# Order of the upper FFN products, of their PSUM banks and of their weight transfers in a fused attention and SwiGLU kernel

## The chip, the cores and the metric

The kernel runs on one core of one Trainium2 chip. The time is the device time of one execution in microseconds (us). The core's engines work from queues of their own: TensorE (PE; its weight loads are listed as PEld), VectorE (DVE), ScalarE (ACT), GpSimd (POOL) and SyncE (SP). GpSimd computes almost nothing here; it issues most of the transfers between the chip's memory (DRAM) and the on-chip memory (SBUF). Results of TensorE go to PSUM, of which this kernel uses eight banks.

## The reference

```
q, k, v: (4, 8, 768, 64); proj: (64, 6); w_gate, w_val: (512, 1536); w_out: (1536, 512)
q_bucket, k_bucket = 6 sign bits of q @ proj, k @ proj
scores = q @ k.T / 8 where the buckets agree, else -1e9
attn = softmax(scores) @ v                        # (4, 8, 768, 64)
x = attn.transpose(0, 2, 1, 3).reshape(3072, 512)
g = x @ w_gate
out = (g * sigmoid(g) * (x @ w_val)) @ w_out      # (3072, 512), float32
```

The FFN weights come as float64 (seen by the kernel as pairs of 32-bit words) and are narrowed on the chip.

## The kernel before

**Attention.** The work is cut into 16 pairs of heads (4 batches of 4), and each pair into two halves of 384 query columns. A half is a unit: first a score section of 36 matmuls (`score`, L491: for each of six key chunks and each of two heads two passes of the float32 product and one product of hash signs that does the masking), with 12 exponentials on ScalarE (L494), then 24 matmuls with `v` (`attend`, L506). VectorE adds the exponentials for the denominators (L520, L524). `norm` (L557) scales the finished rows of x later.

**FFN, upper part.** While the attention of one batch runs, the FFN of the batch before is put between its units, some atoms after each. `up_strassen` multiplies x (512 by 768 tokens) with w_gate and w_val in blocks. One call of `both(i)` is a block of work here: it makes two of the twelve column tiles of the hidden layer, for gate (g = 0) and value (g = 1). It uses the Strassen-Winograd form: seven products n = 0 to 6 for each g, with weights A11, S1, S2, A12, S3, S4 and A22, that accumulate on PSUM banks: n = 0, 2, 4, 6 on bank a, n = 1, 5 on bank b, n = 3 on bank c. Gate and value have a bank each, so there are a0, a1, b0, b1 (0 for gate, 1 for value). A product is four matmul instructions of 384 columns. After n < 3 ScalarE copies the bank to SBUF (L660), after n = 3, 4, 5 VectorE adds the bank to that copy (`plus`, L585), and after n = 6 the bank itself is the result. What is complete goes through `finished`: for the gate a tanh on ScalarE (L567) and a combination on VectorE (L568), for the value the gating on VectorE (L572). These wait in the list `later` for one or two steps (`settle`). After n = 6 they read the PSUM bank directly, after n = 5 the copy in SBUF.

**Nested blocks.** In batches 1 to 3 (`nested`) the product n = 3 is itself done by seven inner products of 192 columns (`deeper`, in four calls go = 0 to 3, on banks c, d and e), with inner weights that `weigh` makes on VectorE from A12. The calls go = 2 and go = 3 accumulate on d and each is read by VectorE. A batch has six blocks; batch 0 (not nested) runs them in the first part of the span, batches 1 and 2 between units, batch 3 in one go at the end.

**Order of work.** The order is written out by hand: `todo` lists the products of each step, `step(at)` issues a step, and each engine runs its queue in that order. Banks come from a pool of seven (`bank`), shared by score sections, upper blocks and down products.

**Weights.** In batch 0 the weights are still being prepared. `load_words` (L278) has GpSimd fetch 512 KB pieces of w_gate, w_val and later w_out; `scale_to` (L293, L294) works on them on ScalarE, `narrow` (L307, L309, L312) on VectorE; `form` makes the sums S1 to S4 (L341) and stores the seven blocks of a tile in DRAM: A11 and A12 (L333), A22 (L335), and the sums in two stores per tile (L345). `bring` (L323) fetches the blocks of a tile for its use into `places[g]`: go = 0 fetches S2, S1, A11, go = 1 the other four. `free` calls it as soon as the products that read the old blocks are done, so each transfer waits in GpSimd's queue for TensorE. Steps of preparation are put between the steps of the blocks (`prepare_on`, `scale_ahead`).

**FFN, down part.** `down_strassen` multiplies the hidden layer with w_out, on banks named c, b, a; its sums of hidden tiles (L585) for a batch's first chunk are begun ahead of the last upper step (`early`).

Of the kernel before, what the change touches and what calls it, by code (L numbers as in the profile page):

```python
# [18 lines left out]
def kernel(  # L19
# [11 lines left out]
    nc = tc.nc  # L31
# [3 lines left out]
    P = 128  # L35
# [157 lines left out]
    NB4 = PIECE // P  # L193
    BL = 2 * P
    NB = 7
    PARTS = [slice(0, 3), slice(3, NB)]
    S2, S1, A11, A12, S3, S4, A22 = range(NB)
    ram = [dram.tile([P, NB, BL], FP32, tag=f"ram{i}", name="ram") for i in range(NG)]
    STAGE = NJ * PIECE
    PAD = 4 * AW - NFP * HD  # L200
# [26 lines left out]
    formed = part(8 * BL, at=down_at).rearrange("p (g x m) -> p g x m", g=2, m=BL)  # L227
# [90 lines left out]
    def bring(k, go):  # L318
        if k < B * NG:
            if k < NG:  # L320
                while k not in summed:
                    next(preparing)
            nc.gpsimd.dma_start(places[k % 2][:, PARTS[go], :], ram[k % NG][:, PARTS[go], :])  # L323

    def form(n):

        blocks = stages[n % 2].rearrange("p k (g r m) -> p g k r m", g=2, m=P)
        a11, a12, a21, a22 = (blocks[:, :, 2 * k : 2 * k + 2, r, :]
                              for r in range(2) for k in range(2))
        group = [n // 2 * NB4 + 2 * pair + n % 2 for pair in range(2)]  # L330
        for pair, i in enumerate(group):
            w = stages[n % 2][:, :, 2 * pair * P : 2 * (pair + 1) * P]
            nc.gpsimd.dma_start(  # L333
                ram[i][:, A11 : A12 + 1, :].rearrange("p n (j m) -> p (n j) m", m=P), w[:, :, 0:P])
            nc.gpsimd.dma_start(ram[i][:, A22, :].rearrange("p (j m) -> p j m", m=P),  # L335
                                w[:, 2:4, P : 2 * P])
        s2, s1, s3, s4 = (formed[:, :, x, :].rearrange("p g (j m) -> p g j m", m=P)
                          for x in range(4))
        for o, x, y, op in ((s3, a11, a21, ALU.subtract), (s2, a22, s3, ALU.subtract),
                            (s1, s2, a11, ALU.add), (s4, a12, s2, ALU.subtract)):  # L340
            nc.vector.tensor_tensor(o, x, y, op=op)  # L341
            yield True
        for pair, i in enumerate(group):
            for at, x in ((S2, 0), (S3, 2)):
                nc.gpsimd.dma_start(ram[i][:, at : at + 2, :], formed[:, pair, x : x + 2, :])  # L345
            summed.add(i)
            if i < 2:
                for go in range(2):
                    bring(i, go)

    def prepare():
# [235 lines left out]
    def up_strassen(x, b, first):  # L587
# [16 lines left out]
        nested = b > 0  # L604
# [5 lines left out]
        def both(i):  # L610


            f = 2 * i
            k0 = b * NG + 2 * i
            now = [{}, {}]
            later = []
            done = [set(), set()]
            inner = {}

            def tile_of(g, spot):  # L620
                m, half = spot
                t = gate_tile() if g == 0 else hidden(f + m, half)
                now[g][spot] = t
                return t

            def settle(at):
                while later and later[0][0] <= at:
                    later.pop(0)[1]()

            def finished(g, spot, c, at, wait):  # L630
                if g == 0:
                    then = gate(tile_of(0, spot) if spot not in now[0] else c, c)
                else:
                    then = lambda: gated(hidden(f + spot[0], spot[1]), now[0][spot], c)
                later.append((at + wait, then))

            def free(g, n):
                done[g].add(n)
                if done[g] >= {0, 1, 2} and n in (0, 1, 2):
                    bring(k0 + 2 + g, 0)  # L640
                if len(done[g]) == NB:
                    bring(k0 + 2 + g, 1)

            def outer(n, g, at):
                my = now[g]
                block, to, xs = (
                    (A11, "a", [x[j][:, lo] for j in range(2)]),
                    (S1, "b", [x[j][:, hi] for j in range(2)]),
                    (S2, "a", [t2[:, j] for j in range(2)]),
                    (A12, "c", [x[2 + j][:, lo] for j in range(2)]),  # L650
                    (S3, "a", [t3[:, j] for j in range(2)]),
                    (S4, "b", [x[2 + j][:, hi] for j in range(2)]),
                    (A22, "a", [t4[:, j] for j in range(2)]),
                )[n]
                w = places[g][:, block, :].rearrange("p (j m) -> p j m", m=P)
                c = my[to]
                product(c, [(w[:, j], xs[j]) for j in range(2)], n in (0, 1, 3))
                spot = ((0, 0), (1, 1), (0, 1), (0, 0), (1, 1), (0, 1), (1, 0))[n]
                if n < 3:
                    nc.scalar.copy(tile_of(g, spot), c)  # L660
                elif n < 6:
                    plus(my[spot], my[spot], c)
                    c = my[spot]
                settle(at)
                if n >= 3:
                    finished(g, spot, c, at, 1 if n == 6 else 2)
                free(g, n)

            v11, v12, v21, v22 = (places[g][:, A12, j * P : (j + 1) * P]
                                  for g in range(2) for j in range(2))
            r1, r2, r3 = (inner_w[:, k] for k in range(3))
            r4 = v21

            def weigh():
                for o, p, q, op in ((r3, v11, v21, ALU.subtract), (r2, v22, r3, ALU.subtract),
                                    (r1, r2, v11, ALU.add), (r4, v12, r2, ALU.subtract)):
                    plus(o, p, q, op)

            def deeper(go, at):
                tg, tv = now[0][0, 0], now[1][0, 0]
                for w, to, xs, start, t, part in (
                    ((v11, "d", xl[:, 0], True, tg, 0), (r1, "e", xl[:, 1], True, tv, 1),
                     (v12, "c", xr[:, 0], True, tg, 0)),
                    ((r2, "d", u2, False, tg, 1), (r4, "e", xr[:, 1], False, tg, 1)),
                    ((r3, "d", u3, False, tv, 1),),
                    ((v22, "d", u4, False, tv, 0),),
                )[go]:
                    c = inner[to]  # L690
                    product(c, [(w, xs)], start)
                    t = t[:, part * HH : (part + 1) * HH]
                    plus(t, t, c)
                if go == 1:
                    finished(0, (0, 0), tg, at, 2)
                if go == 3:
                    finished(1, (0, 0), tv, at, 2)
                    for g in range(2):
                        free(g, 3)


            order = (0, 3, 1, 2, 4, 5, 6) if b == 0 and i == 0 else range(NB)
            todo = [[(n, g)] for n in order if n != 3 or not nested for g in range(2)]
            if nested:
                for go in range(4):
                    todo[6 + go].append(go)

            def step(at):
                if at == 0:
                    if nested:  # L710


                        names = [(inner, "d"), (now[0], "b"), (now[1], "b"), (now[0], "a"),
                                 (now[1], "a"), (inner, "e"), (inner, "c")]
                        for where, name in names:
                            where[name] = bank("up")[:, 0 : HH if where is inner else HQ]
                    else:
                        for name in "cba":
                            for w in range(2):
                                now[w][name] = bank("up")[:, 0:HQ]  # L720
                    while first:
                        first.pop(0)()
                if nested and at == 4:
                    weigh()
                for what in todo[at]:
                    if isinstance(what, tuple):
                        outer(*what, at)
                    else:
                        deeper(what, at)
                if at == len(todo) - 1:  # L730
                    settle(at + NB)

            for at in range(len(todo)):
                size = 2 if nested and at in (6, 7) else 1
                atoms.append((size, lambda at=at: step(at), at == len(todo) - 1))
# [103 lines left out]
    for u in range(0, N, NCH):  # L839
        n, half, _ = units[u]  # L840
# [103 lines left out]
```

## Time and profile before

The median of three runs is 998.54 us (998.32 to 999.62); the profiled execution spans 998.8 us.

| stretch, us | what runs | PE busy | DVE busy | ACT busy | DMA share |
|---|---|---|---|---|---|
| 0 to 106.9 | attention of batch 0, weights | 104.36 | 87.17 | 91.36 | 0.78 |
| 106.9 to 287.7 | attention of batch 1, upper FFN of batch 0, weights | 176.90 | 150.92 | 91.70 | 0.60 |
| 358.3 to 526.5 | attention of batch 2, upper FFN of batch 1 | 168.20 | 100.69 | 68.06 | 0.36 |
| 601.0 to 769.2 | attention of batch 3, upper FFN of batch 2 | 168.20 | 100.72 | 68.07 | 0.32 |
| 833.7 to 940.9 | upper FFN of batch 3 alone | 107.20 | 52.57 | 29.30 | 0.28 |
| 940.9 to 998.8 | down FFN of batch 3 alone | 54.78 | 16.96 | 4.47 | 0.08 |

The stretches left out are down products, partly beside attention. Busy times are us within the stretch. A busy TensorE row says that matmuls were in flight, not that they followed each other at full pace, so the time of a section of equal work is the better measure. In the profile's lines, a tile is named by the program's names: `up` and `po` are banks of the upper and down products, `sc` of the scores, `room` is the large SBUF tile with the weights, `ram` the formed weights in DRAM, `c` and `hid` the gate and hidden tiles.

### The profile page before, as it was taken

How to read it: one execution, taken by the hardware profiler on the slowest of the kernel's cores; microseconds unless marked ns; L12 is line 12 of the kernel's file. 1: busy time of each engine (PE TensorE's matmuls, PEld its weight loads, DVE VectorE, ACT ScalarE, POOL GpSimd, SP SyncE). 2: the span in 40 equal slices, each digit the busy share in tenths (PEclk: the TensorE clock that was granted, in tenths of full speed). 3: DMA queues.
4: the chain of work that ended last, by engine and by line, in shares of the span. 5: the costliest groups of instructions: out<-in, count | busy, mean ns of one | idle time of the engine just before them, and what ended most of it. 6: DMA issues, size and time to landing. Idle time of an engine off the chain costs nothing.

```text
span 998.8 us, 12932 instructions
## 1 busy us (share of the span) xinstructions
PE 989.2 (99%) x4705; PEld 618.0 (62%) x4705; DVE 608.8 (61%) x1066; ACT 397.3 (40%) x885; POOL 107.6 (11%) x212
## 2 busy tenths in 40 slices
PE   9999999999999999999999999999999999999998
PEld 4444555455576775556557776565556787666687
DVE  5898888678973625666564554655667442545531
ACT  7999555366323214444342223334443211222200
POOL 3222233131000000000000000000000000111000
PEclk9999999999999999999999999999999999999999
DMA  8777585786213033423331304233212011332101
GB/s 234 225 250 222 156 262 173 202 271 162 77 50 76 22 85 108 93 82 99 99 96 33 70 17 117 80 91 108 74 59 77 22 37 53 115 107 77 39 28 37
DMA packets 120944, 106.98 MB, mean 107 GB/s; under 512 B 89456, under 2 KB 104272, under 8 KB 120880
## 3 DMA queue, kind: packets, MB, share of 16 engines
q0 software_dynamic: 19296, 73.28, 22.7%
q1 hardware_dynamic: 100784, 32.67, 14.1%
q8 instruction: 37, 0.61, 0.2%
q10 hardware_dynamic: 800, 0.20, 0.1%
q14 instruction: 27, 0.22, 0.1%
HBM read 81.79 MB, written 17.30 MB: 99 GB/s over the span
## 4 chain that ended last, share of the span: by engine, by line
PE 91%; DVE 2%; ACT 2%; DMA 2%; issue 1%; POOL 0%; DVEq 0%; ACTq 0%; POOLq 0%
PE up L581 41%; PE po L581 22%; PE sc L491 15%; PE av L506 11%; DMA room<-in_moe_w_out_dram 1%; PE sum L537 1%; PE hps L409 1%; DVE acc L524 1%; PE tps L393 1%; ACT A L494 1%; ACT room L494 0%; DMA proj<-in_proj_dram 0%; DVE room L365 0%; ACT kb L414 0%; DVE c L568 0%
## 5 line engine op out<-in xcount | busy, mean ns | idle before, releaser
L581 PE MATMUL up<-xT,room 128*128 128x384 f32 (+1 forms) x732 | 238.0, 465 | 0.0
L581 PE MATMUL up<-xc,room 128*128 128x384 f32 x576 | 197.4, 486 | 0.0
L581 PEld LDWEIGHTS up<-xT,room 128*128 128x128 f32 x732 | 135.3, 190 | 82.9 <-issue 9.8
L491 PE MATMUL sc<-qT,kT 64*128 64x384 f32 x768 | 166.8, 499 | 3.7 <-DVE c L568 3.7
L581 PEld LDWEIGHTS up<-xc,room 128*128 128x128 f32 x576 | 108.4, 190 | 66.8
L585 DVE TENSOR_TENSOR c<-c,up 128x192 f32<-128x192 f32 (+1 forms) x126 | 53.4, 435 | 131.8 <-PE up L581 129.5
L524 DVE TENSOR_TENSOR acc<-acc,A 128x768 f32<-128x768 f32 x128 | 122.6, 958 | 17.2 <-ACT A L494 4.6
L323 POOL DMA_DIRECT2D room<-ram x96 | 51.8, 540 | 712.1 <-PE up L581 689.2
L491 PEld LDWEIGHTS sc<-qT,kT 64*128 64x128 f32 x768 | 75.8, 188 | 56.1 <-issue 39.9
L494 ACT ACTIVATE A<-sc 128x384 f32<-128x384 f32 x256 | 105.4, 503 | 5.8 <-PE sc L491 5.4
L789 ACT COPY o<-po 128x256 f32<-128x256 f32 x48 | 17.9, 372 | 200.7 <-PE po L581 200.7
L567 ACT ACTIVATE th<-c 128x384 f32<-128x384 f32 x72 | 37.6, 522 | 150.8 <-DVE c L568 112.9
L506 PE MATMUL av<-A,vraw 128*64 128x384 f32 (+1 forms) x512 | 88.2, 486 | 0.0
L585 DVE TENSOR_TENSOR o<-o,po 128x256 f32<-128x256 f32 x36 | 15.1, 420 | 106.5 <-PE po L581 78.4
L491 PE MATMUL sc<-qb,kb 64*128 64x384 bf16 x384 | 72.8, 325 | 0.5 <-DVE kb L423 0.5
L581 PE MATMUL po<-wo,hid 128*128 128x256 f32 x288 | 67.2, 382 | 0.0
L581 PE MATMUL po<-wo,room 128*128 128x256 f32 x288 | 66.3, 379 | 0.3 <-DVE room L585 0.3
L581 PE MATMUL po<-room,hid 128*128 128x256 f32 x288 | 66.1, 379 | 0.0
L506 PEld LDWEIGHTS av<-A,vraw 128*64 128x64 f32 x512 | 36.7, 137 | 46.0 <-issue 44.6
L494 ACT ACTIVATE room<-sc 128x384 f32<-128x384 f32 x128 | 53.9, 493 | 25.5 <-PE sc L491 25.2
L581 PEld LDWEIGHTS po<-wo,hid 128*128 128x128 f32 x288 | 54.0, 190 | 12.5 <-issue 4.9
L660 ACT COPY c<-up 128x384 f32<-128x384 f32 x72 | 34.5, 479 | 68.0 <-PE up L581 68.0
(122 smaller groups left out, 1070.3 us busy)
## 6 DMA issues: line engine op xcount, KB each, us to landing
room<-ram POOLq DMA_DIRECT2D x48, 512.0 KB, 4.7
room<-ram POOLq DMA_DIRECT2D x48, 384.0 KB, 4.0
ram<-room POOLq DMA_DIRECT2D x36, 256.0 KB, 4.7
vraw<-in_v_dram SPq DMA_DIRECT2D x16, 384.0 KB, 3.2
out_dram<-o SPq DMA_DIRECT2D x48, 128.0 KB, 1.7
room<-in_moe_w_out_dram POOLq DMA_DIRECT2D x10, 512.0 KB, 7.6
qraw<-in_q_dram SPq DMA_DIRECT2D x48, 96.0 KB, 3.0
hid<-in_moe_w_gate_dram POOLq DMA_DIRECT2D x9, 512.0 KB, 6.6
```

The costliest lines, as they stand in the source:

```text
L323: nc.gpsimd.dma_start(places[k % 2][:, PARTS[go], :], ram[k % NG][:, PARTS[go], :])
L393: nc.tensor.transpose(ps[:, i * P : (i + 1) * P], raws[name, n][:, half * CH + i, :, :].rearrange("p h d -> p (h d)"), ident)
L409: nc.tensor.matmul(tile_[i * BLOCK : (i + 1) * BLOCK, 0:HQ], hash_w, T[name, n][:, half * HQ : (half + 1) * HQ], start=True, stop=True)
L491: nc.tensor.matmul(sc[h], x["k", n][rows, ks], x["q", n][rows, qs], start=start, stop=not start)
L494: nc.scalar.activation(weights(u)[:, h, 0:HQ], sc[h], AF.Exp, scale=SCALE * (OFF / 2 if n <= NP else 1.0))
L506: nc.tensor.matmul(ps[h * D : (h + 1) * D, 0:width], raws["v", n][:, h, c, :], a[:, h, 0:width], start=c == 0, stop=c == NCH - 1)
L524: nc.vector.tensor_tensor(acc[n, half], acc[n, half], a[:, :, 0:HQ], op=ALU.add)
L567: nc.scalar.activation(th, g, AF.Tanh, scale=0.5)
L581: nc.tensor.matmul(ps, a, x, start=start and i == 0, stop=i == len(pairs_) - 1, skip_group_check=True)
L585: nc.vector.tensor_tensor(o, a, b, op=op)
L660: nc.scalar.copy(tile_of(g, spot), c)
L789: nc.scalar.copy(o, c)
```

## The change

1. The order of the products becomes 0, 1, 2, 3, 4, 6, 5 (in the very first block 0, 3, 1, 2, 4, 6, 5): n = 6, which closes bank a, is no longer last; n = 5 on bank b is. The purpose is that a block ends with a bank that one VectorE addition sets free.
2. The four inner calls, which stood after the products of steps 6, 7, 8 and 9, stand ahead of those of steps 6, 7, 9 and 11, so that the last two lie two steps apart. `weigh` is issued at step 5 in place of 4.
3. The blocks of a tile are laid out anew in DRAM and SBUF, so that the four sums are contiguous and go to DRAM by one transfer per tile in place of two.
4. A tile's blocks are fetched by three transfers in place of two: S1, S2, A11; A22, S3, S4; and A12 by itself. In batch 0 the first one waits for the product n = 3 as well.

```diff
-    PARTS = [slice(0, 3), slice(3, NB)]
-    S2, S1, A11, A12, S3, S4, A22 = range(NB)
+    PARTS = [slice(3, 6), slice(0, 3), slice(6, NB)]
+    A22, S3, S4, S1, S2, A11, A12 = range(NB)
...
-        s2, s1, s3, s4 = (formed[:, :, x, :].rearrange("p g (j m) -> p g j m", m=P)
+        s3, s4, s1, s2 = (formed[:, :, x, :].rearrange("p g (j m) -> p g j m", m=P)
                           for x in range(4))
...
         for pair, i in enumerate(group):
-            for at, x in ((S2, 0), (S3, 2)):
-                nc.gpsimd.dma_start(ram[i][:, at : at + 2, :], formed[:, pair, x : x + 2, :])
+            nc.gpsimd.dma_start(ram[i][:, S3 : S2 + 1, :], formed[:, pair, :, :])
             summed.add(i)
             if i < 2:
-                for go in range(2):
+                for go in range(3):
                     bring(i, go)
...
             def free(g, n):
                 done[g].add(n)
-                if done[g] >= {0, 1, 2} and n in (0, 1, 2):
-                    bring(k0 + 2 + g, 0)
-                if len(done[g]) == NB:
-                    bring(k0 + 2 + g, 1)
+                for go, ns in enumerate(({0, 1, 2} if nested else {0, 1, 2, 3}, {4, 5, 6}, {3})):
+                    if n in ns and done[g] >= ns:
+                        bring(k0 + 2 + g, go)
...
-            order = (0, 3, 1, 2, 4, 5, 6) if b == 0 and i == 0 else range(NB)
+            order = (0, 3, 1, 2, 4, 6, 5) if b == 0 and i == 0 else (0, 1, 2, 3, 4, 6, 5)
             todo = [[(n, g)] for n in order if n != 3 or not nested for g in range(2)]
             if nested:
-                for go in range(4):
-                    todo[6 + go].append(go)
+                for go, at in enumerate((6, 7, 9, 11)):
+                    todo[at].insert(0, go)
...
-                if nested and at == 4:
+                if nested and at == 5:
                     weigh()
```

## Prediction before the run

> **What bounds the kernel now.** I read the page's shares, then the chain that ended last in order of time, then the list of waits, then the timelines of single engines where the chain leaves TensorE.
>
> ```profile
> PE 989.2 (99%) x4705; PEld 618.0 (62%) x4705; DVE 608.8 (61%) x1066; ACT 397.3 (40%) x885; POOL 107.6 (11%) x212
> ...
> PE 91%; DVE 2%; ACT 2%; DMA 2%; issue 1%; POOL 0%; DVEq 0%; ACTq 0%; POOLq 0%
> ```
>
> TensorE owns the span, so only time in which it is held back can be won. The chain shows where that is (start, length, what):
>
> ```profile
> 135.72 18.26 PE up L581 x56
> ...
> 173.05 9.82 DMA room<-in_moe_w_out_dram
> 182.89 0.66 ACT wo L293
> 183.56 0.55 ACT room L294
> 184.54 0.57 DVE c L568
> ...
> 210.33 5.06 DMA room<-in_moe_w_out_dram
> ...
> 432.24 5.05 PE sc L491 x36
> ...
> 460.72 5.33 PE sc L491 x29
> ...
> 516.62 5.92 PE sc L491 x35
> ...
> 833.88 107.14 PE up L581 x372
> ```
>
> An undisturbed score section takes 5.05 us. After the third and fourth FFN blocks of batch 0 it takes 10.01 (181.26 to 191.26) and 7.20 (214.97 to 222.17), after the fifth and sixth 5.46 and 5.65. In batches 1 and 2 four take 5.33 and the two after a batch's last block 5.92. An upper block by itself: two matmuls of 384 columns start 0.323 apart, of 192 columns 0.162; 48 and 14 of them make 17.75 us, and 107.14/6 is 17.86.
>
> ```profile
> POOL room L323 <- PE up L581: 689.2, 81, 90.5
> ...
> ACT wo L293 <- DMA room<-in_moe_w_out_dram: 12.2, 3, 6.3
> ...
> PEld up L581 <- DVE hid L585: 7.7, 18, 0.5
> ```
>
> The first line is idle GpSimd. The second is ScalarE standing in front of a w_out transfer that hasn't landed; the tanh behind it, VectorE's gate and the PSUM bank follow. The third occurs once per nested block, 18 times: the last inner product waits for VectorE to read bank d.
>
> GpSimd's queue in the third block:
>
> ```profile
> 169.79 2.20 POOL L345 DMA_DIRECT2D ram<-room  x4
> 171.98 1.08 POOL L323 DMA_DIRECT2D room<-ram  x2
> 173.05 0.54 POOL L278 DMA_DIRECT2D room<-in_moe_w_out_dram  x1
> ```
>
> The w_out load of 173.05 stands behind four stores of sums and two weight transfers. VectorE after a batch's last block:
>
> ```profile
> 516.79 0.55 DVE L585 TENSOR_TENSOR room<-hid 128x384 f32<-128x384 f32 x1
> 517.37 0.56 DVE L585 TENSOR_TENSOR room<-room,hid 128x384 f32<-128x384 f32 x1
> 517.85 0.55 DVE L585 TENSOR_TENSOR hid<-hid 128x384 f32<-128x384 f32 x1
> 518.32 1.02 DVE L572 SCALAR_TENSOR_TENSOR hid<-c,hid 128x384 f32<-128x384 f32 x2
> 519.25 0.55 DVE L568 SCALAR_TENSOR_TENSOR c<-c,up 128x384 f32<-128x384 f32 x1
> ```
>
> The last line is the read that frees bank a; three sums for the down product and two gatings run before it, and the scores wait until 519.86.
>
> [...] TensorE reads 99% busy through sections of 5.05 and 5.92 us with equal work. [...] the load took 9.82 us here against a median of 7.6. [...] in the trace the two weight transfers of 171.98 and 172.52 landed at 178.72 and 180.04, the load at 182.87. [...]
>
> **The change, part by part.** PSUM banks pass on in the order in which they were let go: in the last stretch a block begins at 851.57 although the last read of bank a ends at 852.93, so it took an older bank. Hence the score section's first two pairs of banks are old, and today's a0 comes sixth. With S4 (n=5) last, the order becomes c, e, a0, b0, a1, d, b1: the late ones come later, and b0 and b1 need only one add (0.55), no tanh and gate.
>
> *a. Score sections of batches 1 and 2.* I lay out a block from the durations above, zero at its first product. TensorE: A22 (n=6) at 12.05 to 13.34 and 13.66 to 14.95, S4 ends at 16.2 and 17.86. VectorE with its `norm` of 1.0 (L557): gate on a0 done by 15.9, add on b0 by 16.95, gating on a1 by 17.4, add on d by 17.7, on b1 by 18.65. The scores start at 17.95 and need a0 and b0 at 18.85, a1 and d at 19.65, b1 at 20.5. So nothing waits: 4 x 0.28 = 1.1 us saved. In the two 5.92 sections the three sums (1.65) go ahead of the adds on d and b1: d at 19.35, b1 at 19.9, still in time. 2 x 0.87 = 1.7 saved.
>
> *b. Inner steps spaced out.* The last inner product comes two steps after the read of d. Saves 12 x 0.10 + 6 x 0.03, which are the gaps before that product in the timeline: 1.4 us. Moving `weigh` one step costs nothing: it needs 1.15 us, has 1.29 of step 5 and its operands have landed earlier.
>
> *c. Down product after the last block.* The gated tile (0,0) now comes behind three sums and the two adds: 20.9, while the down product reads it at 20.1. It waited 0.19 (943.02 to 943.21), then 0.8: +0.6.
>
> *d. Sums by one store.* Two GpSimd instructions fewer per form of 0.55, 12 in all; the bytes are the same. Only in the third and fourth blocks is somebody behind them.
>
> *e. A12 by its own transfer.* 144 in place of 96 transfers, 48 x 0.54 = 26 us more of GpSimd, which idles 89%: no cost by itself. What matters is place. In batch 0 the first part now waits for n=3 too, so it is issued in steps 6 and 7, not 4 and 5. In the third block the w_out load (step 5) passes it: issued at about 171.6, when its L312 ends, and landing after the stores (177.8) plus 1.5 to 2.8 us, the spacing that 512 KB had here: 180.6. ScalarE scales until 181.9, tanh of A22 182.4, gate on a0 183.05. Score tile 4 needs a0 at 182.1: a stall of 1.0 in place of 4.96, so -4.0. Bounds: 4.96 saved if it lands by 179.5, 1.9 if it still lands at 182.87 (then only the missing second tanh and the later banks help).
>
> In the fourth block the load (step 6) passes one of the two transfers, 256 KB fewer ahead at 211 KB/us: about 1.2 us earlier. But VectorE's preparation there doesn't move up by the full 4 us, since its adds of 0.96 are tied to the exponentials. I take -0.7; bounds -2.15 and 0. In the fifth block the second load (step 7) gets four transfers ahead where it had two: landing up to 1 us later, +0.4. Sixth: the three sums hold b1, and VectorE's L365 follows anyway: 0.
>
> *f. One step between S3 and A22 on bank a in batch 0* (was three). VectorE's adds on S3 end at 12.5 to 13.0 and 13.8 to 14.4 in the six blocks; A22 starts at 13.0 and 14.3. Two of them are late: +0.25. In nested blocks (10.85 against 12.05) none.
>
> Sum: -1.1 - 1.7 - 1.4 + 0.6 - 4.0 - 0.7 + 0.4 + 0.25 = -7.65. 998.5 - 7.65 = 990.9; I say 991.
>
> **The rivals.** *The preparation is limited by the transfers themselves.* For it: DMA share 0.60 over 106.9 to 287.7, near 1 from 170 to 182; a load that starts earlier shares engines with the narrow q and k transfers. Against: the landings come in queue order. Then e gives -0.5 in all, and the total is -3.6 + 0.25 - 0.5 + 0.4: 995.
>
> *Slower.* Loads behind four transfers bring new waits of ScalarE. Two more like that of 210.33 (2.5 each, for the fourth and fifth block), half of the 12 pairs S3 and A22 late by an add (3.3), nothing gained in the third block, a and b kept: 998.5 + 5 + 3.3 - 3.6 = 1003. For it: ScalarE already stands three times for these loads, VectorE is 83% busy in this stretch (150.9 of 180.8). Against: only the second load of blocks four and five goes back, and the former isn't used before 222.9.
>
> **How the numbers follow.** Forecast 0.65, 995 case 0.22, slower 0.13. The range 987 to 997 reaches from the full release of the third and fourth blocks (4.96 + 2.15, and the 3.6 of a to c: 987.8) to the 995 case with f at three times its size and one new ScalarE wait of 1.5 us; it leaves out the slower case and little else. Faster by over 0.2% (2 us): all but little of the forecast, and most of the second: 0.82. Same 0.08, slower 0.10.
>
> **What would show it.** Score sections of 5.05 throughout batches 1 and 2; a block of the last stretch near 17.75; the third block's load issued before its weight transfers, and its score section at 6 us; 5.5 to 7 for the fourth; no L585 wait of the weight loads. The first down product of the last stretch waits near 0.8. Wrong would make it: a w_out load landing no earlier than 182.9, a new line of ScalarE waiting for DMA, gaps before A22 in batch 0, or d and b1 needed sooner after a batch's last block than I place them.

## The result, and the profile after

The changed kernel takes 992.85 us (median of four runs, 991.92 to 994.85), the kernel before 999.08 beside it (998.32 to 1000.34): a ratio of 0.9939, with a 95% interval of 0.992 to 0.9958. Forecast were 991.0 us and a range of 987 to 997. The profiled execution of the changed kernel spans 989.9 us. Most line numbers of the kernel shift by one: L581 is now L580, L491 L490, L585 L584, L572 L571, L568 L567, L345 L344.

The shares of the page: TensorE is busy 6.5 us less, GpSimd 19.0 us more, for 36 more instructions.

```profile
PE 982.7 (99%) x4705; PEld 613.0 (62%) x4705; DVE 607.6 (61%) x1066; ACT 396.3 (40%) x885; POOL 126.6 (13%) x248
```

The chain that ended last, in order of time (start, length, what), with the score sections of the third, fourth and fifth block of batch 0, then one of batch 1:

```profile
181.43 5.04 PE sc L490 x36
...
191.92 18.37 PE up L580 x56
210.29 5.59 PE sc L490 x36
...
231.28 6.99 DMA room<-in_moe_w_out_dram
238.29 0.67 ACT wo L293
238.95 0.56 ACT room L294
239.91 0.57 DVE c L567
240.95 4.00 PE sc L490 x26
...
455.04 5.05 PE sc L490 x36
```

The w_out load has left the third and fourth section, where it stood in the chain before, and has come into the fifth.

The list of waits (in total, times, longest) says the same: ScalarE still stands three times for w_out, but for 8.5 us in place of 12.2. The wait of TensorE's weight loads for the additions (L585, now L584), 7.7 us in 18 times before, is gone from the nested blocks. Five new ones, 2.1 us in all, stand in its place; the timeline has them in the second, fourth and sixth block of batch 0.

```profile
POOL room L323 <- PE up L580: 663.5, 73, 90.2
...
ACT wo L293 <- DMA room<-in_moe_w_out_dram: 8.5, 3, 3.8
...
PEld up L580 <- DVE c L584: 1.1, 3, 0.5
PEld up L580 <- DVE hid L584: 1.0, 2, 0.6
```

GpSimd's queue in the third block. Two stores of sums stand ahead of the load, where four stores and two weight transfers did before, and the load is issued at 170.98, not 173.05. The two stores fewer make 1.07 us of this, the two weight transfers, which now follow the load, 1.08:

```profile
169.62 1.13 POOL L344 DMA_DIRECT2D ram<-room  x2
170.98 0.53 POOL L278 DMA_DIRECT2D room<-in_moe_w_out_dram  x1 [0.23 <-issue]
171.50 0.55 POOL L323 DMA_DIRECT2D room<-ram  x1
```

It lands at 178.92 in place of 182.87, and the scores start at 181.43.

VectorE around the end of batch 1's last block; the scores start at 510.53:

```profile
508.95 0.56 DVE L584 TENSOR_TENSOR c<-c,up 128x384 f32<-128x384 f32 x1 [0.37 <-PE up L580]
509.42 0.55 DVE L571 SCALAR_TENSOR_TENSOR hid<-c,up 128x384 f32<-128x384 f32 x1
509.89 0.55 DVE L584 TENSOR_TENSOR room<-hid 128x384 f32<-128x384 f32 x1
...
511.42 0.81 DVE L584 TENSOR_TENSOR hid<-hid,up 128x192 f32<-128x192 f32 x2
512.14 0.55 DVE L567 SCALAR_TENSOR_TENSOR c<-th,c 128x384 f32<-128x384 f32 x1
```

The bank that is read at 508.95 is set free by that one add; the gating of a1 (509.42) is done before the sums begin. Only the adds of 511.42 come behind the three sums, and nobody waits for them: the section takes 5.04, where it took 5.92.

Stage by stage, between the two profiles (lengths of the same stretches of TensorE's work):

| place | before | after | difference |
|---|---|---|---|
| third section of batch 0 | 10.01 | 5.05 | -4.96 |
| fourth | 7.20 | 5.59 | -1.61 |
| fifth | 5.46 | 6.76 | +1.30 |
| sixth, and the down chunk after it | 24.50 | 24.13 | -0.37 |
| upper blocks of batch 0 (three of six) | 54.78 | 55.32 | +0.54 |
| other score sections, batches 1 and 2 | 4 x 5.33, 2 x 5.92 | 6 x 5.05 | -2.88 |
| nested blocks, last stretch included | 323.15 | 321.73 | -1.42 |
| last down stretch | 57.94 | 58.45 | +0.51 |

That is -8.9, and the medians differ by 6.2. The profiled run of before took 1000.88 us, 1.8 above the median; that of after took 991.92, 0.9 below its own. These two make up the 2.7, and where the runs' spread comes from is the first thing that the experiments found. The sections of batch 0 also differ between two traces of one kernel: a second trace of before has 9.23, 7.01 and 5.83 for the third to the fifth, a second one of after 5.05, 5.38 and 6.92.

### The profile page after: what moved, and what is told of

Its sections match the earlier page's. It is cut to its first block, busy times and chain, and to the rows that moved or that the text cites. A ratio compares the mean times of both kernels' runs of the same rounds, so it can differ in the third digit from the quotient of the medians.

```text
span 989.9 us, 13051 instructions
## 1 busy us (share of the span) xinstructions
PE 982.7 (99%) x4705; PEld 613.0 (62%) x4705; DVE 607.6 (61%) x1066; ACT 396.3 (40%) x885; POOL 126.6 (13%) x248
## 4 chain that ended last, share of the span: by engine, by line
PE 92%; DVE 3%; issue 2%; ACT 1%; DMA 1%; POOL 1%; DVEq 0%; POOLq 0%; ACTq 0%
PE up L580 42%; PE po L580 22%; PE sc L490 14%; PE av L505 11%; PE sum L536 1%; PE hps L408 1%; DMA room<-in_moe_w_out_dram 1%; PE tps L392 1%; DVE room L364 0%; PE idle L135 0%; DVE acc L523 0%; DMA room<-ram 0%; ACT A L493 0%; ACT kb L413 0%; DVE hid L571 0%
## 5 line engine op out<-in xcount | busy, mean ns | idle before, releaser
L580 PE MATMUL up<-xT,room 128*128 128x384 f32 (+1 forms) x732 | 240.1, 465 | 0.0
L580 PE MATMUL up<-xc,room 128*128 128x384 f32 x576 | 199.9, 487 | 0.0
L580 PEld LDWEIGHTS up<-xT,room 128*128 128x128 f32 x732 | 136.6, 190 | 87.4 <-issue 9.2
L323 POOL DMA_DIRECT2D room<-ram x144 | 77.3, 539 | 679.2 <-PE up L580 663.5
L490 PE MATMUL sc<-qT,kT 64*128 64x384 f32 x768 | 161.1, 495 | 0.7 <-DVE c L567 0.7
L580 PEld LDWEIGHTS up<-xc,room 128*128 128x128 f32 x576 | 107.8, 190 | 62.7 <-DVE c L584 1.1
L584 DVE TENSOR_TENSOR c<-c,up 128x192 f32<-128x192 f32 (+1 forms) x126 | 54.0, 436 | 141.0 <-PE up L580 138.9
L490 PEld LDWEIGHTS sc<-qT,kT 64*128 64x128 f32 x768 | 69.2, 187 | 54.0 <-issue 42.9
L584 DVE TENSOR_TENSOR o<-o,po 128x256 f32<-128x256 f32 x36 | 15.2, 421 | 107.0 <-PE po L580 78.3
L580 PE MATMUL po<-wo,hid 128*128 128x256 f32 x288 | 67.2, 383 | 0.5 <-DVE hid L571 0.5
L490 PE MATMUL sc<-qb,kb 64*128 64x384 bf16 x384 | 66.4, 323 | 0.5 <-DVE kb L422 0.5
L580 PE MATMUL po<-wo,room 128*128 128x256 f32 x288 | 66.4, 380 | 0.5 <-DVE room L584 0.5
L580 PE MATMUL po<-room,hid 128*128 128x256 f32 x288 | 66.1, 379 | 0.0
L580 PEld LDWEIGHTS po<-wo,hid 128*128 128x128 f32 x288 | 54.1, 190 | 12.9 <-issue 4.9
```

Of the source, the lines that this page charges most:

```text
L490: nc.tensor.matmul(sc[h], x["k", n][rows, ks], x["q", n][rows, qs], start=start, stop=not start)
L580: nc.tensor.matmul(ps, a, x, start=start and i == 0, stop=i == len(pairs_) - 1, skip_group_check=True)
L584: nc.vector.tensor_tensor(o, a, b, op=op)
```

## The experiments

Each kernel was timed beside the kernel before; the ratios are to that one. "Theory A" and "Theory B" in the expectations are what the prediction says and its rival.

**Order without transfers, and transfers without order.** order_only has parts 1 and 2 of the change and the old layout, stores and transfers. moves_only has parts 3 and 4 with the old order of products and inner steps.

```diff
# order_only, on the kernel before
-            order = (0, 3, 1, 2, 4, 5, 6) if b == 0 and i == 0 else range(NB)
+            order = (0, 3, 1, 2, 4, 6, 5) if b == 0 and i == 0 else (0, 1, 2, 3, 4, 6, 5)
...
-                for go in range(4):
-                    todo[6 + go].append(go)
+                for go, at in enumerate((6, 7, 9, 11)):
+                    todo[at].insert(0, go)
...
-                if nested and at == 4:
+                if nested and at == 5:
```

> The kernel before with parts 1 and 2 alone (product order, inner steps spaced out, weigh at step 5); stores and weight transfers as before. Theory A (bank order and place in GpSimd's queue both count in the preparation): the upper blocks of batches 1 to 3 win what they won in the changed kernel, 4.2 us less the 0.5 at the last down product; the third block's w_out load still lands near the end of the block, so its score section is about 8.0 us (10.01 before, 5.05 with the whole change), the fourth 6.5 to 7, the fifth at most 5.5 (6.76 with the whole change). In all 993 to 994. Theory B (the order of banks is the whole gain, the transfers add nothing): the third section is 5.05 here too, and the time is that of the whole change, 991 to 993, or 1.3 better for the fifth block.

> The changed kernel with the old product order and inner steps: parts 3 and 4 alone. Theory A: the w_out load of the third block passes two weight transfers, lands about 4 us earlier, and the score section falls from 10.01 to about 5.3; fourth about 6; fifth about 6.7, as its second load now stands behind four transfers. Batches 1 to 3 as before (5.33, 5.92, gaps of 0.10). In all 994 to 995.5. Theory B: nothing, 998.5 to 999.5.

Measured: order_only 997.5 us, ratio 0.9977 (0.9968 to 0.9987); moves_only 997.97, 0.9981 (0.9973 to 0.999). Both gain less than expected, and neither time lies in the range of either theory. In the traces batches 1 and 2 of order_only are those of after, and moves_only has the third section at 5.05 as after has. So in the traces each part acts in the stage where the forecast put it. What holds each back is a stall left in batch 0: order_only has a third section of 9.60 with its load landing at 183.02, 0.15 later than before; moves_only has a fifth of 9.60, with 2.0 us without a matmul. There the load lands 1.4 later than in after (239.70 for 238.26), but the scores go on 2.5 later (243.06 for 240.52): with the old order a combination and a gating on VectorE (L567, L571) stand ahead of the read that frees the bank, where after has none. So where a load is late, the order of products counts in batch 0 as well. The stretches around the stall of order_only's third section, the columns being length, busy time of PE, PEld, DVE, ACT and POOL (with instructions), granted clock of TensorE, DMA share and GB/s:

```profile
183.20:185.30 2.10, 0.10 (x3) 0.04 (x2) 0.65 (x2) 1.42 (x3) 0.81 (x2) 0.98 0.93 304
185.30:188.70 3.40, 3.40 (x13) 2.74 (x15) 3.17 (x6) 2.21 (x6) 0.00 (x0) 0.51 0.93 327
188.70:192.00 3.30, 3.30 (x24) 2.04 (x22) 2.45 (x4) 3.21 (x8) 0.00 (x0) 1.00 0.57 212
```

After 2 us without work TensorE resumes, "busy", and does 13 matmuls in 3.4 us where the next 3.3 us hold 24: the granted clock is 0.51. The kernel before has the same thing in its third section, with a gap of 2.43:

```profile
183.70:186.20 2.50, 0.08 (x1) 0.00 (x0) 1.58 (x3) 2.50 (x7) 0.01 (x1) 0.98 0.93 285
186.20:189.60 3.40, 3.39 (x13) 2.64 (x15) 2.21 (x3) 1.17 (x4) 0.00 (x0) 0.51 1.03 348
189.60:193.00 3.40, 3.40 (x24) 1.76 (x22) 2.55 (x4) 2.46 (x6) 0.00 (x0) 1.00 0.32 112
```

After's fifth section, with a gap of 0.7, keeps the full clock:

```profile
239.80:240.50 0.70, 0.03 (x1) 0.00 (x0) 0.59 (x2) 0.08 (x1) 0.00 (x0) 1.00 0.74 149
240.50:243.90 3.40, 3.38 (x23) 2.71 (x25) 3.19 (x6) 2.88 (x8) 0.00 (x0) 1.00 0.75 250
```

Over the traces of this case, gaps of 1.59, 1.96, 2.0, 2.40 and 2.43 us in batch 0's sections (before_again, moves_only, order_only, spaced_only and before) were each followed by one such stretch. Beside the gap of 3.43 (early_part, below) stand two in a row, 6.8 us, estimated from mean clocks of 0.87, 0.50 and 0.65 in 213.50:217.00, 217.00:220.40 and 220.40:224.00. The gap of 1.25 in before's fourth section brought none (1.00 in 218.00:221.40). One stretch costs about 3.4 x 0.5 = 1.7 us, an estimate from its length and its clock. So before's 4.96 of lost time is 2.43 of gap, 1.7 of slow clock and 0.8 that is left over.

**The same kernel before, once more** (before_again).

> The kernel before, unchanged, for another trace. If the third block's section of 10.01 us holds a stretch of 3.4 us at half clock that comes by chance of where the stall of 2.4 us falls, a run whose mean clock is 1.0 shows the same stall and a section of 8.0 to 8.6, and one at 0.998 shows 9.5 to 10.1. The rival (the half clock is bound to the stall): 10 in either.

Ten runs gave 997.9 to 1002.68 us: four with a mean granted clock of 1.0 over the run have a median of 998.38, five with 0.998 one of 1000.82 (one half-clock stretch is 1.7 of 1000). The traced run was of the second kind, with a gap of only 1.59 and a section of 9.23, a little below the 9.5 to 10.1 expected. No trace of a run at 1.0 was had, so the length of the section in such a run is not shown. The times of before beside the first four experiments split in the same way: 44 at 1.0 with a median of 998.7, 18 at 0.998 with 1001.29. These lie 2.6 apart, 0.9 more than one stretch costs. So runs at 1.0 probably also waited less (an estimate from these numbers), and a gap too short to bring the stretch would explain them as well as chance does; which it is stays open.

**Spacing alone.** spaced_only has part 2 of the change and nothing else.

```diff
-                for go in range(4):
-                    todo[6 + go].append(go)
+                for go, at in enumerate((6, 7, 9, 11)):
+                    todo[at].insert(0, go)
...
-                if nested and at == 4:
+                if nested and at == 5:
```

> The kernel before with part 2 alone: the inner calls at steps 6, 7, 9 and 11 ahead of the products, weigh at step 5; product order and transfers as before. Theory A: the gap of 0.03 to 0.10 before the last inner product is gone in all 18 nested blocks, the last stretch of six blocks is 106.5 in place of 107.14, and 1.4 us are won; but with bank a still closing last and the add on bank d now issued in the last step, the score sections of 5.33 and 5.92 stay or grow by up to 0.3 each. In all 997.5 to 999. Rival: the spacing by itself is what frees the banks, and the sections fall to 5.05 as well: 994.5 to 995.5.

996.93 us, 0.9975 (0.9963 to 0.9987). The nested blocks are those of after, as expected. But the four sections of 5.33 are at 5.05 as well, and the two of 5.92 at 5.41: 2.14 of the 2.88 that the forecast gave to the new bank order. The reason is in VectorE's queue: before, its combination for the first half waits 0.32 for a tanh, probably because of the inner steps ahead of it, and the read that frees bank a starts at 461.95; spaced, there is no such wait and it starts at 460.94: 0.46 after the scores, where it was 1.23 after them. That wait is 0.32 of the 0.77; the timelines also show two gatings right ahead of the read before and one after, and no run takes these apart. The last down stretch is already at 58.33.

The time lies between the ranges of the two expectations. It is also no longer than order_only's 997.5, which has the new order of products besides. Runs at a mean clock of 1.0 alone say the same: 995.44 for spaced_only (7 of 15 runs) and 995.4 for order_only (3 of 19), beside 998.7 for before (44 of 65) and 996.76 for moves_only (11 of 22). So what the new order adds to the spacing is seen in the traces, not in the times.

**When the first weight transfer may go in batch 0.** early_part lets it go without waiting for n = 3; late_part holds both that one and A12's back until n = 6 is done, too. Of the line with the three sets only the sets are shown.

```diff
# early_part
-({0, 1, 2} if nested else {0, 1, 2, 3}, {4, 5, 6}, {3})
+({0, 1, 2}, {4, 5, 6}, {3})
# late_part
-({0, 1, 2} if nested else {0, 1, 2, 3}, {4, 5, 6}, {3})
+({0, 1, 2} if nested else {0, 1, 2, 3, 6}, {4, 5, 6}, {3} if nested else {3, 6})
```

> The changed kernel, but in batch 0 the first weight transfer again doesn't wait for n=3, so it goes out in steps 4 and 5, ahead of the w_out load of the third block. Theory A: that load lands 2 to 3 us later, the third score section is 7 to 8 us in place of 5.05; in the fifth block only the two A12 transfers stand between the loads and its section falls from 6.76 to about 5.5. In all +1 to +2 against the whole change: 994 to 995. Theory B: no difference from the whole change, within 0.5 us.

> The kernel after, with the transfers of two parts of the weights of batch 0's first columns held back until n=6 is summed, so that in the third, fourth and fifth block both w_out loads stand ahead of them in GpSimd's queue. If the place of a load in that queue is what sets the score sections, the fifth block's second load is issued about 2.2 us earlier than at 231.28, the wait of ScalarE of 3.8 at 238.3 goes, and its section falls from 6.76 to about 5.1; the third and fourth stay at 5.05 to 5.6: 1.7 to 2.2 us less than after, 990.5 to 991.5. The rival (the loads land when the engines have room, wherever they stand): no difference from after within 0.5. A third possibility: the weights that now come last are wanted by the scores themselves, and TensorE waits for them at the start of the sections: slower than after by 1 to 3.

early_part: 1001.37 us, 1.0022 (1.0012 to 1.0031), slower than before. Its third section, with the load issued at 172.00 behind two weight transfers, is 6.65; the harm is in the fourth (12.27) and fifth (7.22). GpSimd's queue and the chain in the fourth block:

```profile
201.93 1.08 POOL L344 DMA_DIRECT2D ram<-room  x2
208.62 1.09 POOL L323 DMA_DIRECT2D room<-ram  x2 [5.62 <-PE up L580]
209.71 0.54 POOL L278 DMA_DIRECT2D room<-in_moe_w_out_dram  x1
```

```profile
209.71 5.08 DMA room<-in_moe_w_out_dram
214.83 0.54 issue
215.37 0.64 ACT room L294
216.41 0.57 DVE c L567
217.02 7.19 PE sc L490 x19
```

A weight transfer that waits in the queue holds the load behind it for 5.62 us; in after that load goes out at 206.18. The gap here is 3.43, and 19 matmuls take 7.19, at a granted clock of 0.50 in the first 3.4 us of it and 0.65 in the next 3.6.

late_part: 989.88 us (989.64 to 989.98), 0.9901 (0.9884 to 0.9918). The fifth block's second load is issued at 224.35, ahead of all four transfers:

```profile
224.35 0.53 POOL L278 DMA_DIRECT2D room<-in_moe_w_out_dram  x1 [3.05 <-ACT c L659]
226.52 0.54 POOL L323 DMA_DIRECT2D room<-ram  x1 [1.64 <-PE up L580]
```

In after it stands behind the last of them:

```profile
230.74 0.54 POOL L323 DMA_DIRECT2D room<-ram  x1 [0.22 <-DVE wo L309]
231.28 0.53 POOL L278 DMA_DIRECT2D room<-in_moe_w_out_dram  x1
```

The load lands 3.94 us after its issue, at 228.29; after's took 6.98 and landed at 238.26. The third, fourth, fifth and sixth section are all at 5.04 or 5.05: 2.3 us off the trace, as the first theory said. No wait for the weights takes its place: from 170 to 290 TensorE has work for 119.52 of 120 us.

**After once more** (after_again), beside the next two.

> The kernel after, unchanged, beside the others on the same chip. If the late transfers' gain over it is that of the fifth and fourth section (1.7 and 0.5) and not the chip's, it gives 992 to 993 at a granted clock of 1.0, and 1.7 more in a run with a clock of 0.998. The rival (chips differ by that much): within 0.7 of 989.9.

991.98 us (991.66 to 992.6), 0.9925 (0.9911 to 0.9938): late_part's gain of 2.1 isn't the chip's. On the same chip late_old (below), which differs from late_part in the first block alone, took 989.76 to 990.26.

**The three sums behind the gate.** sums_after issues the last step of the upper block ahead of the sums for the down product; late_sums has this and late_part's edit.

```diff
-        atoms[at] = (size, lambda: (early(), last()), end)
+        atoms[at] = (size, lambda: (last(), early()), end)
```

> The kernel after, with the gate of the upper group put ahead of the three sums for the down product in VectorE's order at the end of a last block. If the first down product of the last stretch is late because its gated tile stands behind three sums of 0.55, the gap of 934.29 falls from 0.7 to under 0.2 and the last down stretch from 58.45 to about 57.9: 0.5 us less than after (992.3). The rival (the sums are what is waited for): no less, or up to 1 more, since the down product then waits for the sums. For the two score sections after the last blocks of batches 0 and 1, nothing (5.05) in the first view.

> The two edits together (weights' transfers behind both loads in batch 0, gate ahead of the three sums). If each acts on a place of its own, the gains add: 2.2 to 2.7 us less than after, 990 to 990.7. If they act on the same wait, no more than the better of the two.

991.68 us (0.9923, 0.9905 to 0.9941) and 989.61 (0.9903, 0.9886 to 0.9919). The wait of the first down product is gone, first in after, then in sums_after:

```profile
931.44 2.32 PE L580 MATMUL po<-wo,hid 128*128 128x256 f32 x10
934.29 0.70 PE L580 MATMUL po<-wo,hid 128*128 128x256 f32 x2 [0.54 <-DVE hid L571]
```

```profile
931.98 2.75 PE L580 MATMUL po<-wo,hid 128*128 128x256 f32 x12
934.66 1.35 PE L580 MATMUL po<-wo,room 128*128 128x256 f32 x5
```

The stretch is 58.09, 0.36 shorter and not the 0.5 expected. The times can't tell either kernel from its fellow without this edit, so the gains don't visibly add. late_sums has the loads of late_part, yet its runs reach from 989.32 to 991.45, and its trace has a second section of 6.19; why was not followed.

**Two stores of the sums.** two_stores is after with part 3's one store split in two of half the size.

```diff
-            nc.gpsimd.dma_start(ram[i][:, S3 : S2 + 1, :], formed[:, pair, :, :])
+            for x in (0, 2):
+                nc.gpsimd.dma_start(ram[i][:, S3 + x : S3 + x + 2, :], formed[:, pair, x : x + 2, :])
```

> The kernel after, with the weights' sums of an upper group stored by two transfers of half the size in place of one. My theory (GpSimd has room, and the place of the loads is set by the order of the parts): 0, within 0.5 us, the load of the third block issued at most 0.6 us later (171.5) and landing at most 0.6 later (179.5), its section 5.05 to 5.7. The rival (the one store is what brought the load forward): the third section back to 7 or more, 2 to 5 us slower than after.

993.99 us, 0.9944 (0.9928 to 0.9961): 1.1 to 2.0 above the two measurements of after, more than the 0.5 expected, though their ratios overlap. The third block's load is issued at 173.84 and lands at 181.04; third and fourth section take 5.67 and 6.27. Of the 2.9 us by which it is issued later, only 0.53 lie between the first store of the blocks (L333) and the load; that store itself begins 2.3 later (168.25 for 165.92). 0.6 of this is already there when the upper blocks begin (107.48 for 106.87), as in late_old (107.38), whose stores are those of after. What delays it by the rest was not followed.

**The one step between S3 and A22 in batch 0.** late_old and late_first put the old order back in batch 0, on top of late_part.

```diff
# late_old
-            order = (0, 3, 1, 2, 4, 6, 5) if b == 0 and i == 0 else (0, 1, 2, 3, 4, 6, 5)
+            order = (0, 3, 1, 2, 4, 5, 6) if b == 0 and i == 0 else (0, 1, 2, 3, 4, 6, 5)
# late_first
+            order = ((0, 3, 1, 2, 4, 5, 6) if b == 0 and i == 0
+                     else range(NB) if b == 0 else (0, 1, 2, 3, 4, 6, 5))
```

> The kernel with the late transfers in batch 0, and in batch 0 alone the old order of upper groups (the last product on bank a, three steps after S3 instead of one); batches 1 and 2 keep the new order. If the one step between S3 and A22 costs the 0.54 us that the upper blocks and what follows showed, and the new order brings batch 0's score sections nothing that the loads don't already bring, this is 0.5 less than the late transfers alone: 989.3. The rival (the new bank order also spares the score sections of batch 0 their own wait, 0.28 as in batches 1 and 2, and the sixth 0.6): four or five sections lose 0.3 to 0.6 each, 990.5 to 991.5, slower than the late transfers alone.

> The kernel with the late transfers in batch 0, and in all six blocks of batch 0 the old order of upper groups (the last product on bank a, three steps after S3 instead of one). The edit before this one (late_old) meant to do that, but it reached the first block alone. If the one step between S3 and A22 is what the upper blocks of 18.39, 18.37 and 18.56 and the down chunk of 19.08 showed, these go back to 18.26 and 18.85, 0.77 us. Against it stand the score sections: after a last product on bank a they wait for the gate, 0.28 to 0.6 each in six sections, as the two of 5.65 and 5.46 before the change did: 1.5 to 3 us. Net 0.7 to 2.2 slower than the late transfers alone, 990.6 to 992.1. The rival (in batch 0 the sections are ruled by the loads alone): all stay at 5.05, and the time is 0.8 less, 989.1.

late_old gave 989.82 us, but its edit reaches the first block only (b and i both zero), not batch 0 as its expectation says, so it tells nothing of the question. late_first: 989.76 us, 0.9895 (0.9879 to 0.9912). The upper blocks are back at 18.26 (-0.54 in all), the down chunk at 18.33 (-0.75), the first five sections stay at 5.05, and the sixth goes to 6.31 (+1.26). It comes out even with late_part. So with loads in time the new order itself gains nothing in batch 0 but the sixth section, which it pays for with the steps that are too close; the other five sections don't need it then.

The fastest kernels here are late_part and the three built on it, at 989.6 to 989.9, not to be told apart.

## Why the prediction was right, step by step

**a, score sections of batches 1 and 2:** -2.8 forecast, -2.88 measured, all six at 5.05. The size is right, the reason only in part: spacing alone brings 2.14, and the new order the other 0.74, which the times don't show.

**b, inner steps:** -1.4 forecast, -1.41 measured, and it needs nothing but the spacing.

**c, first down product:** +0.6 forecast, +0.51 measured; its wait is 0.54, where 0.8 was forecast. Putting the sums behind the gate removes that wait and 0.36 of the stretch. The spacing alone already costs 0.39, so the queue of sums isn't the only way to it.

**d, one store:** nothing forecast; between -1 and -2 by the times of two_stores, not settled. The two stores fewer are half of the load's earlier issue in the third block (1.07 of 2.07), and somebody does stand behind them there, as the forecast itself says.

**e, place in GpSimd's queue:** the mechanism holds. The load passes the weight transfers and is issued at 170.98, where 171.6 was forecast; early_part, which moves it back behind them, loses more than the whole change gains. The sizes were off. Third section -4.96 for -4.0: the load landed 1.7 earlier than the 180.6 forecast, before the bound of 179.5 at which the forecast saw the whole 4.96 come back. The forecast also took these 4.96 us for pure waiting, and 1.7 of them were half clock, which only some runs have. Fourth -1.61 for -0.7; fifth +1.30 for +0.4, by the second load behind four transfers, which the forecast named; sixth section and down chunk -0.37 for 0. Nor are the 4.96 the work of the place alone. With the new order of products the third section is 9.60 (order_only); with the one store besides and the weight transfers still ahead 6.65 (early_part, which also has A12's own transfer); with these behind the load and two stores 5.67 (two_stores); with both 5.05. Either brings most of it by itself, and the forecast gave all to the place.

**f, one step between S3 and A22 in batch 0:** +0.25 forecast, +0.54 measured: five of the twelve pairs are late (the five new waits for L584), where two were foreseen. Gaps before A22 in batch 0 were named as a sign of being wrong; they came, at this small size. late_first, which takes the step back, takes just this away.

The terms sum to -8.9 for the -7.65 forecast, and the median fell by 6.2; beside after_again it is 7.8 (999.8 to 991.98), and the interval of the first ratio, 0.992 to 0.9958, is a gain of about 4 to 8 us. The forecast subtracted terms read in one trace from a median of other runs, and the trace had a half-clock stretch of 1.7 us that most runs lack. What in the end hit the time within 1.9 us was thus in part luck, two errors of opposite sign: e came out 1.3 larger in the traces, and the trace of before stood 1.8 above its median.

**The rivals.** "Limited by the transfers themselves" falls: late_part changes nothing but when the weight transfers may go, and with that the order in GpSimd's queue, and its loads land and sections shrink as the order says. "Slower" falls for the change, but early_part at 1001.37 shows how near it lay: its new waits were real, and the condition on n = 3 is what keeps them out.

## What to carry to other kernels

In a queue whose entries wait for an engine in order, an early, long-waiting entry delays the urgent one behind it (5.62 us in early_part); place a load that somebody stands for ahead of transfers that will wait for TensorE, and count what stands ahead of it, stores too, in every block, not in one. Before taking a stall from a profile as a saving, compare the profiled run's own time with the median, and look at the clock after the stall. When two edits are made together, try the simpler one alone: here spacing gave most of what the reordering was credited with.

## What the hardware showed that was not expected

A gap of 1.59 to 2.43 us in TensorE's work was followed by 3.4 us at half the clock (0.51 in before), at a further cost of about 1.7 us by the estimate above, and beside one of 3.43 stood 6.8 us of it; after the gap of 1.25 the clock was 1.00. In before's record of the clock the slow stretch is 3.413 us long. It doesn't begin with the end of the gap: in moves_only the gap ends at 243.06, and the mean clocks of 1.00 in 239.00:243.30 and 0.68 in 243.30:246.80 put the fall at about 244.6, an estimate. In the records of before and after all changes of the clock lie whole multiples of 3.413 us apart: in before 180.906 us (53 times) from the change at 5.2 us to the fall, 3.413 to the rise and 808.959 (237 times) from there to the fall behind the last product; in after 986.452 (289 times) from the change at 5.4 us to that last fall. In the 3.4 us that ended with the fall in these sections, TensorE stood idle for 1.6 to 2.5 us: 2.34 in before, the others estimated from the gaps and the mean clocks of the windows. What brings the fall, and whether a gap between 1.25 and 1.59 us does, was not shown.

late_part, which has no gap above 0.5 us in this part, has runs within 0.34 us of each other, where before's spread over 4.6 us in the same series; late_sums, whose six runs all have a mean clock of 1.0, spreads over 2.1 us, so these stretches are not the only source of spread.
